# Second feed-forward layer: drains on VectorE, a longer planned way for the scale of x, seven block products from the third tile

## The chip, the cores and the metric

The kernel runs on one core of one Trainium2 chip. The metric is device time in microseconds, the median of several executions. TensorE multiplies, VectorE and ScalarE read its results from PSUM, GpSimd works on SBUF alone, and SyncE (SP) issues nearly all transfers.

## The reference, cut to what matters

```python
x = attention(q, k, v)                     # 2304 tokens x 512, fp32
h = x @ w_in;  x = (silu(h)) @ w_out       # first layer, 512 -> 2048 -> 512
h = x @ w_in2                              # second layer, the one that changes
g = np.maximum(h, 0.0) + alpha * np.minimum(h, 0.0)
out = (g @ w_out2).astype(np.float32)
```

## The kernel before

The second layer takes the 2304 tokens in nine tiles of 256 (n = 0 to 8). A tile has eight steps; a step makes 256 of the 2048 hidden values. Every fp32 operand is split into a high and a low fp16 part, and a product of two operands is three fp16 matmuls (function `three`, line 1030).

For one step, `up2` does 24 matmuls of 256 columns into one PSUM bank h (four such banks take turns: h, h, acc, acc). `act2` turns h into g: VectorE makes u (lines 1199 and 1203), ScalarE copies it to the high part of g (by the helper `act`, line 325), VectorE subtracts for the low part (line 1224). u has two buffers. `down2` multiplies g by the output weights and accumulates over the eight steps.

`down2` has two forms. The plain form (`down_plain`) takes the four 128x512 products of a step, 12 matmuls of 512 columns, into two banks. The other form (`factor`) splits g and the weights into 2x2 blocks and forms the block product from seven products in place of eight: 21 matmuls of 256 columns into four banks called e, e, s, o. It needs sums of blocks of u, four more operations on GpSimd in `act2` (line 1211), a g of 7 blocks in place of 4, and mixed output weights, which `mix_o` makes once for all tiles: a load of the kept weights by SP, four GpSimd operations (line 434), one on ScalarE and one on VectorE (line 386). The constant `PLAIN` is the first tile of the seven-product form.

At the end of a tile `store2` empties the banks ("drains" them) into the SBUF tile osb, scaled, and SP stores it. In the seven-product form that is one ScalarE copy of 256 columns and then seven VectorE operations (line 1319), each adding a bank half to osb. The plain form drains two banks, one on ScalarE and one on VectorE (line 1271). A new tile's first down needs the banks of the tile before it.

`load2` brings the next tile's x: four loads by SP into the single buffer xs, a VectorE maximum over it (line 1136), and then a maximum over the partitions. From tile 2 on that takes two transfers: `row` writes 128 single values to DRAM, `rows` reads them back to all partitions, and VectorE reduces `rows` (line 1146). After some tiny operations ScalarE and VectorE split x (line 1157) into xh, of which there are two.

Tiles 0 and 1 go through the eight steps together, while the output weights are split and kept; the others follow one by one, with the next tile's ups running some steps ahead of a tile's downs.

The order of all instructions on all engines is made ahead of time by a planner (class `Plan`). Each operation has an engine, a cost and a due time `at` in the planner's own units; the planner simulates the engines and always takes, of the operations that can start, the one with the smallest `at`. A tile buffer's turn and the dependences set what can start. The engines then work through their lists strictly in order. A transfer's planned end is:

```python
            if e == "DMA":
                dma_free = max(dma_free, start + min(o.cost, 0.63) + 0.65) + o.extra
                o.end = dma_free + 0.95
```

where the cost is 0.5 and `extra` the size in KB divided by 350. In `act2` and `down2` due times advance by `STEP2` = 0.85 a step.

Of the kernel before, what the change touches and what calls it, by code (L numbers as in the profile page):

```python
# [13 lines left out]
AF = mybir.ActivationFunctionType  # L14
ALU = mybir.AluOpType
# [21 lines left out]
FIRST_LOAD = (-20.0, -6.9)  # L37
EYE = -19.85
AHEAD = 4
DOWN2, STEP2, STEP_FIRST, G_PLACES = 3.0, 0.85, 1.8, 3  # L40
TOGETHER2, PLAIN, FIRST_DOWN = 2, 3, 1.8


SLACK, SPARE2, SWITCH = 0.56, 0.3, 1.0
# [188 lines left out]
def dve2_cost(n, pointers=0, shared=False):  # L233
    return (155 + 60 * pointers + n / 0.96) * (1.1 if shared else 1.0) * 1e-3
# [15 lines left out]
def block_causal_attention_silu_prelu(  # L250
# [14 lines left out]
    nc = tc.nc  # L265
# [3 lines left out]
    NT, DM = out.shape  # L269
# [6 lines left out]
    N2 = NT // T2  # L276
    assert (S, DM, PAIRS) == (576, 512, 4)

    plan = Plan()
    add = plan.add  # L280
# [6 lines left out]
    psum = ctx.enter_context(tc.tile_pool(name="psum", bufs=1, space=PSUM))  # L287
# [28 lines left out]
    def dma(dst, src, kib, reads=(), writes=(), after=()):  # L316
        return add("DMA", 0.5, lambda: nc.sync.dma_start(dst(), src()), reads, writes, kib / 350.0, after)
# [809 lines left out]
    def load2(n, after=()):  # L1127
        s = sb(ff2_p, [128, T2 // 32, KD, 32], F32, "xs")
        x2 = x2d[places[n]]
        for z in range(4):  # L1130
            add("DMA", 0.5, lambda z=z: nc.sync.dma_start(
                s()[32 * z:32 * z + 32].rearrange("p i k t -> p i (k t)"),
                x2()[:, 128 * z:128 * z + 128].rearrange("(i p) n -> p i n", p=32)),
                [x2], [(s, z)], extra=T2 / 350.0, after=after)
        sc = xsc[n] = sb(ff2_p, [128, 4], F32, "xsc", 3)
        add("DVE", dve_cost(KD * T2), lambda: nc.vector.tensor_reduce(  # L1136
            sc()[:, 0:1], s().rearrange("p i k t -> p (i k t)"), axis=AX.X, op=ALU.max, apply_absolute_value=True),
            [s], [sc])
        if n < TOGETHER2:
            spread(lambda: sc()[:, 0:1], [sc], lambda: sc()[:, 1:2], [sc])  # L1140
        else:
            row = sb(dram_p, [1, 128], F32, f"row{n}")
            rows = sb(ff2_p, [128, 128], F32, "rows")
            dma(lambda: row().rearrange("o p -> p o"), lambda: sc()[:, 0:1], 1, [sc], [row])
            dma(lambda: rows(), lambda: row().to_broadcast([128, 128]), 64, [row], [rows])
            add("DVE", dve_cost(128), lambda: nc.vector.tensor_reduce(sc()[:, 1:2], rows(), axis=AX.X, op=ALU.max),
                [rows], [sc])
        m = lambda: sc()[:, 1:2].bitcast(I32)
        tiny(m, m, 0x7F800000, None, ALU.bitwise_and, None, sc)
        tiny(m, m, float(27 << 23), float(TOP << 23), ALU.max, ALU.subtract, sc)  # L1150
        add("DVE", dve_cost(6), lambda: nc.vector.reciprocal(sc()[:, 2:3], sc()[:, 1:2]), [sc], [sc])
        t = sb(ff2_p, [128, 2, KD, T2], F16, "xh2", 2)
        for kk in range(KD):
            part = lambda e, kk=kk: t()[:, e, kk].rearrange("p (i t) -> p i t", t=32)
            act(T2, lambda part=part: part(0), lambda kk=kk: s()[:, :, kk], AF.Copy, [s, sc], [(t, (0, kk))],
                scale=lambda: sc()[:, 2:3])
            add("DVE", dve_cost(T2, 1, 1), lambda part=part, kk=kk: nc.vector.scalar_tensor_tensor(  # L1157
                part(1), s()[:, :, kk], sc()[:, 2:3], part(0), op0=ALU.mult, op1=ALU.subtract),
                [s, sc, (t, (0, kk))], [(t, (1, kk))])
        for kind in "io":  # L1160
            if kind in wsc:
                add("DVE", dve_cost(1, 1, 1), lambda kind=kind: nc.vector.tensor_scalar(
                    sc()[:, 1:2], sc()[:, 1:2], wsc[kind]()[:, 2:3], 2.0**(G_EXP if kind == "i" else 0),
                    op0=ALU.mult, op1=ALU.mult), [sc, wsc[kind]], [sc])
        tiny(lambda: sc()[:, 3:4], lambda: sc()[:, 1:2], -1.0, None, ALU.mult, None, sc)
        xh2[n] = t
# [99 lines left out]
    def store_plain(n):  # L1266
        sc = xsc[n]
        e = sb(ff2_p, [128, 2, DM], F32, "osb", 2)
        for t, a in enumerate(acc.pop(n)):
            if t:  # L1270
                add("DVE", dve2_cost(DM, 1), lambda a=a: nc.vector.tensor_scalar(
                    e()[:, 1], a(), sc()[:, 1:2], None, op0=ALU.mult), [a, sc], [(e, t)])
            else:
                act(DM, lambda: e()[:, 0], lambda a=a: a(), AF.Copy, [a, sc], [(e, t)], psum=True,
                    scale=lambda: sc()[:, 1:2])
            row = 0
            for r0, count in rows_of(2 * places[n] + t):
                dma(lambda r0=r0, count=count: out[r0:r0 + count],
                    lambda row=row, count=count, t=t: e()[row:row + count, t], count * 2, [(e, t)])
                row += count  # L1280
# [18 lines left out]
    def store2(n):  # L1299
        if n < PLAIN:  # L1300
            return store_plain(n)
        sc = xsc.pop(n)
        banks = acc.pop(n)
        e = sb(ff2_p, [128, 2, DM], F32, "osb", 2)
        c11, c12, c21, c22 = ((j, half) for j in range(2) for half in range(2))
        at = lambda c: lambda: e()[:, c[0], 256 * c[1]:256 * c[1] + 256]

        def part(i):
            bank, half = SLOTS_OF[i]
            return (banks[bank], half), lambda: banks[bank]()[:, 256 * half:256 * half + 256]  # L1310

        key, m1 = part(0)
        act(256, at(c11), m1, AF.Copy, [key, sc], [(e, c11)], psum=True, scale=lambda: sc()[:, 1:2])
        for i, col, base, dst in (
            (5, 1, c11, c22), (3, 3, c22, c21), (4, 1, c22, c12), (4, 1, c21, c22), (2, 1, c11, c11), (1, 3, c21, c21),
            (6, 3, c12, c12),
        ):
            key, m = part(i)
            add("DVE", dve2_cost(256, 1), lambda m=m, col=col, base=base, dst=dst: nc.vector.scalar_tensor_tensor(  # L1319
                at(dst)(), m(), sc()[:, col:col + 1], at(base)(), op0=ALU.mult, op1=ALU.add),  # L1320
                [key, sc, (e, base)], [(e, dst)])
            for j in range(2):
                if i != {0: 6, 1: 1}[j]:
                    continue
                row = 0
                for r0, count in rows_of(2 * places[n] + 1 - j):
                    dma(lambda r0=r0, count=count: out[r0:r0 + count],
                        lambda row=row, count=count, j=j: e()[row:row + count, j], count * 2,
                        [(e, c) for c in ((c11, c12), (c21, c22))[j]])
                    row += count  # L1330
# [3 lines left out]
    for k, j in enumerate(jobs):  # L1334
        start = START[k] if k < len(START) else 2.0 * (k - PAIRS) - LEAD
        for t, f in j.steps():
            at = start + t
            if k < FIRST * PAIRS and t == LOAD:
                at = FIRST_LOAD[k // PAIRS] + 0.1 * k
# [106 lines left out]
    for s in range(half + 1):  # L1446
        base = total + 1 + STEP_FIRST * s
        if s < half:
            for m in order2[2 * s:2 * s + 2]:
                plan.at = base - 1.0  # L1450
                load_w(1, "o", m, scanned)
                plan.at = base
                split_w(1, "o", m)
            for n in range(TOGETHER2):
                plan.at = base + 0.4 * n
                up2(n, s)
                act2(n, s)
            if s == 3:
                load2(TOGETHER2, after=stores[-2:])
        elif low_parts:  # L1460
            low_parts.pop()(())
        if s:
            for n in range(TOGETHER2):
                plan.at = base + FIRST_DOWN + 0.4 * n
                down2(n, s - 1)
    for n in range(TOGETHER2):
        store2(n)
    for k in range((N2 - TOGETHER2) * half + 1):
        n, s = divmod(k, half)
        n += TOGETHER2  # L1470
        base = after_first + STEP2 * k
        if n < N2:
            plan.at = base
            up2(n, s)
            act2(n, s)
            if n == TOGETHER2:
                plan.at = base + 1.0
                mix_o(s)
            if s == 1 and n + 1 < N2:
                load2(n + 1)  # L1480
        elif low_parts:
            low_parts.pop()(())
        if k >= 1:
            pn, s = divmod(k - 1, half)
            plan.at = base + DOWN2 + (SWITCH - 0.4 * s if s < 3 else 0.0)
            down2(pn + TOGETHER2, s)
            if s == half - 1:
                store2(pn + TOGETHER2)

    with tc.manual_schedule():  # L1490
# [86 lines left out]
```

## Time and profile before

| | |
|---|---|
| median of 3 runs | 913.66 us (913.22 to 916.06) |
| the profiled execution | 913.75 us |
| its span, first to last instruction | 912.0 us |
| TensorE busy | 97% of the span |
| VectorE, ScalarE, GpSimd busy | 76%, 51%, 29% |
| mean granted TensorE clock | 0.996 of 2.4 GHz |

The profile is of one execution, and its times count from the first instruction. The second layer's matmuls begin at about 529 us. A busy share is an average over the whole span; what a change in the second layer is worth has to be read from that stretch. Matmul ends in the trace are modelled, so a pace is read from start to start.

### The profile page before, as it was taken

How to read it: one execution, taken by the hardware profiler on the slowest of the kernel's cores; microseconds unless marked ns; L12 is line 12 of the kernel's file. 1: busy time of each engine (PE TensorE's matmuls, PEld its weight loads, DVE VectorE, ACT ScalarE, POOL GpSimd, SP SyncE). 2: the span in 40 equal slices, each digit the busy share in tenths (PEclk: the TensorE clock that was granted, in tenths of full speed). 3: DMA queues.
4: the chain of work that ended last, by engine and by line, in shares of the span. 5: the costliest groups of instructions: out<-in, count | busy, mean ns of one | idle time of the engine just before them, and what ended most of it. 6: DMA issues, size and time to landing. Idle time of an engine off the chain costs nothing. (4 is left out here: it accounts for less than half of the span.)

```text
span 912.0 us, 18221 instructions
## 1 busy us (share of the span) xinstructions
PE 885.8 (97%) x6845; PEld 741.3 (81%) x6845; DVE 694.3 (76%) x1557; ACT 465.2 (51%) x1070; POOL 263.5 (29%) x380
## 2 busy tenths in 40 slices
PE   7899999999999999999999999999989999999997
PEld 5688888898988888889788786667658888888886
DVE  5999767688888888887489897896575856757673
ACT  6987556677868777775236753342122222213121
POOL 6501002232212222221000000572044544536552
PEclk9999999999999999999999999999999999999999
DMA  9952134487665766659698981441110110100010
GB/s 316 407 215 53 35 94 110 110 145 151 123 162 119 155 134 130 151 134 251 222 327 321 268 282 42 142 160 47 27 50 4 47 28 24 28 28 1 24 24 24
DMA packets 134248, 116.55 MB, mean 128 GB/s; under 512 B 100240, under 2 KB 111504, under 8 KB 134160
## 3 DMA queue, kind: packets, MB, share of 16 engines
q1 hardware_dynamic: 133008, 111.19, 44.4%
q0 software_dynamic: 1152, 4.19, 1.1%
q8 instruction: 54, 0.88, 0.5%
q14 instruction: 34, 0.28, 0.1%
HBM read 78.65 MB, written 14.16 MB: 102 GB/s over the span
## 5 line engine op out<-in xcount | busy, mean ns | idle before, releaser
L1030 PE MATMUL h<-x_all,w0i 128*128 128x256 f32 (+1 forms) x1440 | 224.7, 308 | 2.4 <-ACT x_all L325 1.5
L1030 PEld LDWEIGHTS h<-x_all,w0i 128*128 128x128 f32 x1440 | 199.8, 191 | 22.9 <-issue 3.8
L1030 PEld LDWEIGHTS <-w1i 128*128 128x128 f16 x1728 | 168.9, 98 | 24.7 <-issue 0.5
L325 ACT ACTIVATE g<-u 128x896 f16<-128x896 f32 (+1 forms) x72 | 60.7, 843 | 223.6 <-POOL u L1211 112.0
L1030 PEld LDWEIGHTS <-g 128*128 128x128 f16 x1296 | 127.2, 98 | 51.9 <-issue 8.5
L1030 PE MATMUL acc<-w0o,g 128*128 128x512 f32 x672 | 168.8, 394 | 0.2
L1211 POOL TENSOR_TENSOR u<-u 128x128 f32<-128x128 f32 x192 | 116.6, 628 | 162.9 <-DVE u L1203 75.6
L1030 PEld LDWEIGHTS acc<-w0o,g 128*128 128x128 f32 x672 | 122.4, 188 | 27.5 <-issue 2.5
L1030 PE MATMUL acc<-xh,w1i 128*128 128x256 f16 x864 | 100.0, 273 | 0.0
L335 POOL TENSOR_TENSOR g<-t,g 128x512 fp32r<-128x512 f32 x40 | 53.0, 1326 | 161.7 <-ACT g L325 157.7
L1030 PE MATMUL h<-xh,w1i 128*128 128x256 f16 x864 | 99.4, 273 | 0.0
L1224 DVE SCALAR_TENSOR_TENSOR g<-u,g 128x896 f16<-128x896 f32 (+1 forms) x72 | 74.1, 1030 | 12.7 <-ACT g L325 12.6
L325 ACT ACTIVATE p<-p,stat 128x512 f16<-128x512 f32 (+2 forms) x112 | 63.3, 608 | 22.0 <-issue 7.7
L1030 PE MATMUL e<-w1op,g 128*128 128x512 f16 (+1 forms) x336 | 67.6, 333 | 3.9 <-ACT osb L325 2.6
L325 ACT ACTIVATE p<-e,stat 128x256 f32<-128x256 f32 (+2 forms) x98 | 51.0, 527 | 33.2 <-DVE stat L946 22.3
L325 ACT ACTIVATE t<-h 128x512 f32<-128x512 f32 x72 | 43.0, 597 | 44.4 <-PE h L1030 37.7
L1030 PE MATMUL e<-w1om,g 128*128 128x256 f16 x432 | 56.6, 275 | 4.8 <-DVE osb L1319 4.2
L1075 DVE SCALAR_TENSOR_TENSOR t<-t,h 128x512 f32<-128x512 f32 x72 | 49.0, 680 | 13.7 <-ACT t L325 12.5
L325 ACT ACTIVATE g<-t 128x512 fp32r<-128x512 f32 x72 | 45.4, 630 | 19.5 <-DVE t L1075 19.0
L885 DVE SCALAR_TENSOR_TENSOR p<-p,stat,p 128x384 f16<-128x384 f32 (+1 forms) x64 | 48.4, 796 | 4.4 <-ACT p L325 4.1
L1030 PE MATMUL e<-w0o,g 128*128 128x512 f32 x192 | 49.4, 393 | 0.0
L416 POOL DMA_DIRECT2D kept<-wso x8 | 4.8, 602 | 136.2 <-DVE wso L371 70.3
(167 smaller groups left out, 1336.1 us busy)
## 6 DMA issues: line engine op xcount, KB each, us to landing
st<-qkv_b SPq DMA_DIRECT2D x16, 800.0 KB, 4.8
raw0i<-w_in SPq DMA_DIRECT2D x16, 512.0 KB, 9.9
raw0o<-w_out SPq DMA_DIRECT2D x16, 512.0 KB, 9.9
scano<-w_out SPq DMA_DIRECT2D x16, 512.0 KB, 6.6
raw1i<-w_in SPq DMA_DIRECT2D x16, 512.0 KB, 5.3
raw1o<-w_out SPq DMA_DIRECT2D x16, 512.0 KB, 5.9
scani<-w_in SPq DMA_DIRECT2D x13, 512.0 KB, 4.4
x<-x2e SPq DMA_DIRECT2D x18, 256.0 KB, 2.4
```

The costliest lines, as they stand in the source:

```text
L325: nc.scalar.activation(dst(), src(), func, **k)
L335: eng.tensor_tensor(lo(), src(), hi().bitcast(F32), op=ALU.subtract)
L416: add("POOL", 1.5, lambda: nc.gpsimd.dma_start(kept[s](), both().rearrange("p c n -> p (c n)")), [a, b], [kept[s]])
L885: add("DVE", dve_cost(n, 1, 1), lambda hl=hl, rr=rr, pr=pr: nc.vector.scalar_tensor_tensor(hl()[:, :, 1], pr(), rr(), hl()[:, :, 0], op0=A ...
L1030: nc.tensor.matmul(dst, lhs(a), rhs(b), start=(start and n == 0), stop=(stop and n == 2))
L1075: add("DVE", dve_cost(2 * T1), lambda: nc.vector.scalar_tensor_tensor(t(), t(), 1.0, h3(), op0=ALU.add, op1=ALU.mult), [t, h], [t])
L1211: add("POOL", pool2_cost(128, 2.5), lambda out_=out_, x=x, y=y, op=op: nc.gpsimd.tensor_tensor(u()[:, out_], u()[:, x], u()[:, y], op=op), ...
L1224: add("DVE", dve2_cost(blocks * 128, 0, True), lambda: nc.vector.scalar_tensor_tensor(side(1)(), src(), 2.0**-G_EXP, side(0)(), op0=ALU.mu ...
```

## The change

Five things change, all in the second layer.

`PLAIN` goes from 3 to 2, so tile 2 takes the seven-product form. Since it now needs the mixed weights, the calls of `mix_o` move out of the loop over tile 2 and ahead of it, with an earlier due time each (`MIX`).

The transfer `rows` is booked with 2600 KB in place of 64; the transfer itself stays as it is. Only the planner sees the number.

`load2` of the next tile is called at a tile's step 0 and not at step 1.

Every drain is VectorE's: the plain form's ScalarE copy and the first operation of the seven-product form become VectorE operations.

The due times of the drains are 8.0 units (tiles 0 and 1) and 5.0 units (the others) earlier.

```diff
-DOWN2, STEP2, STEP_FIRST, G_PLACES = 3.0, 0.85, 1.8, 3
-TOGETHER2, PLAIN, FIRST_DOWN = 2, 3, 1.8
+DOWN2, STEP2, STEP_FIRST, G_PLACES, MIX = 3.0, 0.85, 1.8, 3, 6.0
+TOGETHER2, PLAIN, FIRST_DOWN = 2, 2, 1.8
...
-            dma(lambda: rows(), lambda: row().to_broadcast([128, 128]), 64, [row], [rows])
+            dma(lambda: rows(), lambda: row().to_broadcast([128, 128]), 2600, [row], [rows])
...
         for t, a in enumerate(acc.pop(n)):
-            if t:
-                add("DVE", dve2_cost(DM, 1), lambda a=a: nc.vector.tensor_scalar(
-                    e()[:, 1], a(), sc()[:, 1:2], None, op0=ALU.mult), [a, sc], [(e, t)])
-            else:
-                act(DM, lambda: e()[:, 0], lambda a=a: a(), AF.Copy, [a, sc], [(e, t)], psum=True,
-                    scale=lambda: sc()[:, 1:2])
+            add("DVE", dve2_cost(DM, 1), lambda a=a, t=t: nc.vector.tensor_scalar(
+                e()[:, t], a(), sc()[:, 1:2], None, op0=ALU.mult), [a, sc], [(e, t)])
...
-        act(256, at(c11), m1, AF.Copy, [key, sc], [(e, c11)], psum=True, scale=lambda: sc()[:, 1:2])
+        add("DVE", dve2_cost(256, 1), lambda: nc.vector.tensor_scalar(
+            at(c11)(), m1(), sc()[:, 1:2], None, op0=ALU.mult), [key, sc], [(e, c11)])
...
                 plan.at = base + FIRST_DOWN + 0.4 * n
                 down2(n, s - 1)
+    plan.at -= 8.0
     for n in range(TOGETHER2):
         store2(n)
+    for s in range(half):
+        plan.at = after_first + STEP2 * s - MIX
+        mix_o(s)
     for k in range((N2 - TOGETHER2) * half + 1):
...
             up2(n, s)
             act2(n, s)
-            if n == TOGETHER2:
-                plan.at = base + 1.0
-                mix_o(s)
-            if s == 1 and n + 1 < N2:
+            if s == 0 and n + 1 < N2:
                 load2(n + 1)
...
             down2(pn + TOGETHER2, s)
             if s == half - 1:
+                plan.at -= 5.0
                 store2(pn + TOGETHER2)
```

## Rows read from the trace of the kernel before

**Rows 1.** The page's first part, TensorE: busy us, share, instructions.

```profile
PE 885.8 (97%) x6845; PEld 741.3 (81%) x6845; DVE 694.3 (76%) x1557; ACT 465.2 (51%) x1070; POOL 263.5 (29%) x380
```

**Rows 2.** Waits of TensorE, 640 to 912 us: total us, times, longest.

```profile
PE e L1030 <- DVE osb L1319: 4.2, 4, 1.5
...
PE e L1030 <- DVE g L1224: 1.3, 1, 1.3
```

**Rows 3.** TensorE's timeline: start, us, instructions; plain and seven-product steps.

```profile
638.88 5.34 PE L1030 MATMUL e<-w1op,g 128*128 128x512 f16 x24
644.06 2.78 PE L1030 MATMUL acc<-xh,w1i 128*128 128x256 f16 x24
...
883.52 0.49 PE L1030 MATMUL e<-w1op,g 128*128 128x256 f16 x3
...
885.81 2.78 PE L1030 MATMUL acc<-xh,w1i 128*128 128x256 f16 x24
```

**Rows 4.** TensorE's timeline at the end of tile 2; in brackets idle time before.

```profile
667.52 0.59 PE L1030 MATMUL e<-w1op,g 128*128 128x512 f16 x2
...
671.58 5.40 PE L1030 MATMUL h<-xh,w1i 128*128 128x256 f16 x48
679.63 0.49 PE L1030 MATMUL e<-w1op,g 128*128 128x256 f16 x3 [2.64 <-ACT osb L325]
...
681.12 1.44 PE L1030 MATMUL e<-w1om,g 128*128 128x256 f16 x6 [0.54 <-DVE osb L1271]
...
683.94 2.78 PE L1030 MATMUL acc<-xh,w1i 128*128 128x256 f16 x24
```

**Rows 5.** The stretch 677 to 684 us: length, busy us by engine, clock, DMA.

```profile
677.00:684.00 7.00, 3.83 (x22) 2.70 (x22) 6.73 (x11) 2.48 (x3) 3.46 (x5) 0.76 0.21 75
```

**Rows 6.** TensorE's timeline at the end of tile 3.

```profile
720.95 0.49 PE L1030 MATMUL e<-w1op,g 128*128 128x256 f16 x3
...
722.07 0.82 PE L1030 MATMUL e<-w1om,g 128*128 128x256 f16 x6 [0.31 <-DVE osb L1319]
...
723.84 2.78 PE L1030 MATMUL acc<-xh,w1i 128*128 128x256 f16 x24
```

**Rows 7.** Waits of VectorE, 540 to 912 us: the longest in total.

```profile
DVE xsc L1146 <- DMA rows<-row: 54.4, 7, 9.9
```

**Rows 8.** Timelines of SP's queue and of VectorE: one scale's way.

```profile
682.41 0.33 SPq L317 DMA_DIRECT2D row<-xsc  x1
...
690.17 0.33 SPq L317 DMA_DIRECT2D rows<-row  x1
...
694.91 0.29 DVE L1146 TENSOR_REDUCE xsc<-rows 128x1 f32<-128x128 f32 x1 [8.30 <-DMA rows<-row]
```

**Rows 9.** Timelines of VectorE and ScalarE near the end of tile 3.

```profile
709.15 0.88 DVE L1199 TENSOR_SCALAR u<-h,alpha_sb 128x256 f32<-128x256 f32 x2
...
715.94 0.88 DVE L1199 TENSOR_SCALAR u<-acc,alpha_sb 128x256 f32<-128x256 f32 x2
...
718.40 0.46 ACT L325 ACTIVATE osb<-e,xsc 128x256 f32<-128x256 f32 x1
718.89 0.49 DVE L1319 SCALAR_TENSOR_TENSOR osb<-e,xsc,osb 128x256 f32<-128x256 f32 x1 [1.35 <-ACT osb L325]
```

**Rows 10.** Timeline of VectorE: the last drain of tile 7.

```profile
881.22 0.47 DVE L1319 SCALAR_TENSOR_TENSOR osb<-s,xsc,osb 128x256 f32<-128x256 f32 x1
```

**Rows 11.** Timelines: last mixed weights, tile 2's first down, GpSimd's first sums.

```profile
621.80 1.28 DVE L386 SCALAR_TENSOR_TENSOR w1om<-v,wsco,w1om 128x1024 f16<-128x1024 f32 x1 [2.01 <-ACT w1om L325]
...
633.67 2.75 PE L1030 MATMUL e<-w1op,g 128*128 128x512 f16 x12
...
668.27 2.60 POOL L1211 TENSOR_TENSOR u<-u 128x128 f32<-128x128 f32 x4 [47.69 <-ACT xh L325]
```

**Rows 12.** Timelines of ScalarE and VectorE at the very end.

```profile
904.68 0.47 ACT L325 ACTIVATE osb<-e,xsc 128x256 f32<-128x256 f32 x1 [3.58 <-PE e L1030]
905.19 1.47 DVE L1319 SCALAR_TENSOR_TENSOR osb<-e,xsc,osb 128x256 f32<-128x256 f32 x3 [2.96 <-ACT osb L325]
```

## The prediction
> **What bounds the kernel now.** I read the page first. TensorE is busy 885.8 of 912.0 us [rows 1], so what can be won is idle time of TensorE, or work of its own. The list of who waited for whom comes next. From 640 us on TensorE waits in only seven places over 0.2 us: four times for VectorE's drains of a finished tile (4.2 us together), once 1.3 us for a VectorE g [rows 2], and at one tile end 2.64 us for a ScalarE drain with 0.54 us for a VectorE one right behind it [rows 4]. All lie at tile ends of the second layer, so I read TensorE's timeline there.
>
> The paces first. In the plain form two down steps take 644.06 − 638.88 = 5.18 us, 2.59 us each; in the seven-product form one takes 885.81 − 883.52 = 2.29 us [rows 3]. The busy figure exceeds the pace by 5.34 − 5.18 = 0.16 us, because the last matmul's modelled end outlasts it; so a row of 48 up matmuls of 5.40 us is 5.24 us of pace, two steps of 2.62.
>
> The end of tile 2, the third tile and today's last plain one, costs twice. Its last down begins at 667.52 and the next work at 671.58: 4.06 us for 2.59 of pace, 1.47 lost. From 671.58 to 683.94 lie two up steps and the first seven-product down: 12.36 − 5.24 − 2.29 = 4.83 lost [rows 3, 4]. Waits explain 2.64 + 0.54 = 3.18 of this; the mean granted clock of 677 to 684 us is 0.76 [rows 5], so part of that stretch ran at the 1.2 GHz level and the rest at 2.4, after TensorE had stood 2.64 us.
>
> The ends of tiles 3 to 6 look alike. At the first of them the down takes 723.84 − 720.95 = 2.89 us, 0.60 over pace, 0.31 of it the listed wait [rows 6]. I take the other 0.29 for each of the four: 4.2 + 4 × 0.29 = 5.36 us. Together the six places lose 1.47 + 4.83 + 5.36 = 11.66 us.
>
> Why are the drains late? VectorE's waits answer: seven times, 54.4 us in all, it stands for the broadcast of x's scale [rows 7]. One case: the row is issued at 682.41, its broadcast at 690.17, and VectorE's reduction runs at 694.91 after 8.30 us idle: a way of 12.5 us [rows 8]. The planner books 0.5 + 0.65 + 0.95 us and KB/350 for a transfer, hence 2.1 + 0.2 + 2.3 = 4.6 us for the way, and so orders the reduction some 8 us too early on an engine that works in order. All u and g work behind it slips. It catches up slowly: two u buffers circulate, and from the u begun at 709.15 to the one begun two steps later at 715.94 it is 6.79 us, 3.4 per step against TensorE's 2.62 + 2.29 = 4.91. A slip of 8.3 us at a gain of 1.5 per step needs some 5.5 steps, 27 us, from 695 to 722: exactly the tile's end, where the drains should run. There ScalarE's first drain comes at 718.40, and VectorE has idled 1.35 us for it at 718.89 [rows 9]. The counter-example is the end of tile 7, during which no x is loaded: the last drain begins at 881.22, TensorE's new down at 883.52, and there is no wait [rows 3, 10].
>
> **Part by part.** *Seven for eight products in tile 2.* Eight down steps save 2.59 − 2.29 each: 2.4 us. The cost is 8 × 2.60 us of GpSimd sums, where GpSimd stood idle 47.69 us; the row that shows this is the first such sum of tile 3. Larger g tiles add 0.3 to 0.4 us per step to ScalarE and VectorE. The mixed weights must be there when tile 2's first down starts, 633.67; today the last of the eight is done at 623.08, and the last is needed only some 35 us after that start [rows 11]. So the order of the eight mixes, brought forward by MIX, is priced at nothing: they run in the first phase already, their eight loads on SP's queue stand ahead of tile 3's x either way, and the cover is at least 10 us. If it were gone, TensorE would wait one for one.
>
> *Longer planned way of the scale.* 2600/350 = 7.43 us are booked for the broadcast, so the way is planned at 0.5 + 0.65 + 0.95 + 0.2 + 0.5 + 0.65 + 7.43 + 0.95 = 11.8 us, against the 12.5 measured. The reduction is then ordered behind two more steps of u and g; of some 8 us per tile about 1 stays, and TensorE's four up buffers, 4 × 4.91 us, cover it. Next late would be x itself, which is loaded nearly two tiles ahead. The transfers planned behind it are shifted in the plan too, but the weights' loads are issued before.
>
> The Trainium skill, "DMA: Bandwidth & Descriptors", section "Anatomy of one DMA — SWDGE (gpsimd) path", speaks against this edit: it gives a DMA about 2.0 us fixed plus bytes/436 GB/s, some 4.2 us for the two as an estimate, which the old plan fits. By it there would be no wait to remove and the sum would end near 905.1; the 12.5 us of this trace decide.
>
> *x a step sooner.* Four x loads, the row and the broadcast go 4.9 us earlier in SP's order, perhaps past the two stores of the tile just ended. SP stands on the row's landing for 7.8 us with the stores behind it; nobody reads these. Priced at nothing, at most 0.2 us.
>
> *Drains on VectorE, five to eight planner units sooner* (a step of 4.91 us is 0.85 units, so 29 to 46 us). ScalarE gives up one 0.46 us drain per tile, VectorE takes it at 0.49 [rows 9], and the hand-over from a ScalarE queue that itself waits for GpSimd's sums disappears. Eight drains at about 0.4 us of pace are 3.3 us; TensorE's two up steps at each end hide 5.24. So I remove all 11.66 us, lower bound nothing, since the drains could stay late. Behind a drain that waits for its product stand the next tile's u and g; four steps of up lead hide that.
>
> The Trainium skill, "VectorE: DVE Perf Modes", section "Specifications", puts ScalarE closer to PSUM, which speaks for leaving it there. By the rows the difference is 0.03 us per drain, 0.2 over the kernel, on an engine that has room.
>
> *The very end.* ScalarE's drain begins at 904.68 and VectorE's next at 905.19 [rows 12]; a VectorE drain of 0.4 us pace in its place ends about there. 0 ± 0.2 us.
>
> **Sum**, from the profiled execution's 913.75 us (span 912.0 and 1.75 around it; the median of the runs is 913.66, so both serve): 913.75 − 11.66 − 2.4 = 899.7. I leave 0.2 us in each of the six places, as no list shows shorter waits: 1.2. Forecast 900.9 us.
>
> **Rivals.**
> 1. *The drains stay late at the four ends* because something else keeps VectorE behind: GpSimd's four sums, which take 2.6 us per step, also sit in the chain of each u buffer, and the new plan may still order drains behind g's that wait for them. For it: those sums are the longest part of the 6.79 us that two steps take with two u buffers [rows 9, 11], and no edit shortens them. Against: tile 7's end, which had the same sums [rows 10]. 899.7 + 5.36 = 905.1; with tile 2's new end as bad as its old one, up to 909.9. Chance 0.21. The page's 2 us rule has its time here, and no more than 0.01 of it.
> 2. *Only the products change:* the planner's order at the ends comes out as before, for example because ready times and not priorities set it. 913.75 − 2.4 = 911.4. Against: the booked way alone changes ready times. Chance 0.08.
> 3. *Slower: VectorE parks on the drains.* With such early priorities a drain is ordered as soon as the plan has its product; where TensorE on the chip is later than in the plan, VectorE stands with all u and g behind it. Today's parks, up to 9.9 us, cost 1.34 us on average at the next end; past the lead of four steps, 19.6 us, every further microsecond stalls TensorE. At 22 us for each of eight drains it costs 8 × 2.4 = 19 us, and with today's losses gone 900 + 19 = 919. Against: TensorE's paces hardly vary. Chance 0.05.
>
> **Numbers.** The forecast has 0.66; its own range is 898.8 (0.9 below the sum, for the very end, the spread of the runs below their median, 0.4, and a better tile 2) to 903. Within 0.3%, 2.7 us, a measurement of this kernel can't tell a change. Taking in most of the first rival, the range is 898.8 to 907.5. Faster by over 0.3% (below 910.9) is the forecast and rival 1, 0.87; within it rival 2, 0.08; slower rival 3, 0.05.
>
> **What would show it.** Tile 2's downs in 256-column matmuls on four banks; VectorE's wait for the broadcast down from 54.4 us to under 15; no ScalarE drain; each tile's eight drains done before the next tile's first down; tile starts 39.3 us apart (8 × 4.91), not 39.3 + 5.36/4 = 40.6; a granted clock of 1.00 from 660 on. It is wrong if TensorE's list of waits still names a drain for over 2 us, or shows a wait for mixed weights in tile 2, or VectorE's list a wait for TensorE's last products of many microseconds.

## The result and the profile after

The changed kernel takes 899.39 us (median of 4 runs, 898.29 to 899.61) against 913.44 us for the kernel before (912.96 to 916.06); the ratio is 0.9838, 95% interval 0.9818 to 0.9858. Forecast were 900.9 us, with 898.8 to 907.5 as the range. The median lies 0.6 us inside the low end; by the ratio, 0.9838 × 913.44 = 898.6 us, it lies 0.2 below it, and the interval of the ratio is 1.8 us wide to either side. The profiled execution took 899.29 us with a span of 897.5.

The page's first part after the change, TensorE (it was [rows 1]):

```profile
PE 879.7 (98%) x6917; PEld 747.7 (83%) x6917; DVE 702.9 (78%) x1572; ACT 463.7 (52%) x1061; POOL 281.6 (31%) x412
```

TensorE is busy for 6 us less, and 72 more matmuls are in the trace: tile 2 does 21 short ones a step for 12 long ones.

To keep the first layer out of the comparison, I use one measure throughout, **the stretch**: from the start of tile 0's first down to the start of the last group of products. In the timeline of TensorE, of the kernel before:

```profile
546.06 2.75 PE L1030 MATMUL e<-w1op,g 128*128 128x512 f16 x12
...
906.44 0.82 PE L1030 MATMUL o<-w1op,g 128*128 128x256 f16 x6
```

and of the changed kernel, with the ends of tiles 2 and 3 between (they answer to [rows 4] and [rows 6]):

```profile
545.62 2.75 PE L1030 MATMUL e<-w1op,g 128*128 128x512 f16 x12
...
667.29 5.40 PE L1030 MATMUL h<-xh,w1i 128*128 128x256 f16 x48
672.53 0.49 PE L1030 MATMUL e<-w1op,g 128*128 128x256 f16 x3
...
674.83 2.78 PE L1030 MATMUL acc<-xh,w1i 128*128 128x256 f16 x24
...
706.59 5.40 PE L1030 MATMUL h<-xh,w1i 128*128 128x256 f16 x48
711.83 0.49 PE L1030 MATMUL e<-w1op,g 128*128 128x256 f16 x3
...
714.13 2.78 PE L1030 MATMUL acc<-xh,w1i 128*128 128x256 f16 x24
...
891.96 0.82 PE L1030 MATMUL o<-w1op,g 128*128 128x256 f16 x6
```

The stretch falls from 360.38 to 346.34 us, by 14.04; the prediction's terms were 11.66 + 2.4 = 14.06. No row of it carries a bracket: TensorE no longer waits over 0.2 us anywhere in the stretch. The first down of tile 4 starts 711.83 − 672.53 = 39.30 us after that of tile 3, eight times 4.91, and takes 714.13 − 711.83 = 2.30 us.

Where [rows 5] had a clock of 0.76, the stretch after tile 2 now reads (length, busy us of TensorE, its weight loads, VectorE, ScalarE, GpSimd, then clock, DMA, GB/s):

```profile
672.00:679.00 7.00, 7.00 (x67) 6.29 (x65) 6.01 (x11) 1.90 (x2) 5.01 (x8) 1.00 0.33 77
```

VectorE's waits from 540 us on (total us, times, longest) have turned around; the wait for the broadcast was 54.4 us in [rows 7]:

```profile
DVE u L1199 <- PE acc L1030: 45.3, 19, 4.3
DVE u L1199 <- PE h L1030: 14.8, 12, 2.3
...
DVE osb L1309 <- PE e L1030: 3.5, 7, 2.5
...
DVE xsc L1146 <- DMA rows<-row: 2.7, 2, 1.5
```

VectorE now waits for TensorE, as the engine that is ahead should. The way of a scale has not become shorter; SP's queue and VectorE's timeline, to be read beside [rows 8]:

```profile
677.72 0.34 SPq L317 DMA_DIRECT2D row<-xsc  x1
684.95 0.34 SPq L317 DMA_DIRECT2D rows<-row  x1
...
691.28 0.28 DVE L1146 TENSOR_REDUCE xsc<-rows 128x1 f32<-128x128 f32 x1
```

The reduction has no bracket: VectorE came to it, 13.6 us after the row's issue, when the data had landed. And the drains of tile 3 (in VectorE's timeline, beside [rows 9]) start with the tile's last products and end before the next down at 711.83:

```profile
705.16 0.48 DVE L1309 TENSOR_SCALAR osb<-e,xsc 128x256 f32<-128x256 f32 x1 [0.17 <-PE e L1030]
...
708.90 0.47 DVE L1316 SCALAR_TENSOR_TENSOR osb<-s,xsc,osb 128x256 f32<-128x256 f32 x1
```

What lies outside the stretch hardly differs: 0.44 us less ahead of it, where TensorE's instructions are the same in both kernels, and 897.5 − 891.96 = 5.54 us behind it against 912.0 − 906.44 = 5.56.

### The profile page after: what moved, and what is told of

It is laid out like the page before. It is cut to its first block, busy times and chain, and to the rows that moved or that the text cites. A ratio compares the mean times of both kernels' runs of the same rounds, so it can differ in the third digit from the quotient of the medians.

```text
span 897.5 us, 18422 instructions
## 1 busy us (share of the span) xinstructions
PE 879.7 (98%) x6917; PEld 747.7 (83%) x6917; DVE 702.9 (78%) x1572; ACT 463.7 (52%) x1061; POOL 281.6 (31%) x412
## 4 chain that ended last, share of the span: by engine, by line
PE 59%; DMA 4%; DVE 3%; SPq 1%; issue 1%; ACT 1%; POOL 0%; DVEq 0%; ACTq 0%
PE h L1030 18%; PE acc L1030 17%; PE e L1030 12%; PE s L1030 5%; PE o L1030 3%; DMA scani<-w_in 2%; PE e L734 2%; PE o L908 1%; SPq L1131 1%; DMA scano<-w_out 1%; DMA xs<-x 1%; DMA raw1o<-w_out 1%; PE s L734 1%; PE o L918 0%; ACT p L325 0%
## 5 line engine op out<-in xcount | busy, mean ns | idle before, releaser
L1211 POOL TENSOR_TENSOR u<-u 128x128 f32<-128x128 f32 x224 | 136.5, 629 | 129.4 <-DVE u L1203 104.5
L325 ACT ACTIVATE g<-u 128x896 f16<-128x896 f32 (+1 forms) x72 | 63.2, 878 | 207.7 <-POOL u L1211 141.3
L1030 PEld LDWEIGHTS <-g 128*128 128x128 f16 x1368 | 133.9, 98 | 32.8
L1224 DVE SCALAR_TENSOR_TENSOR g<-u,g 128x896 f16<-128x896 f32 (+1 forms) x72 | 76.0, 1056 | 12.2 <-ACT g L325 12.2
L1199 DVE TENSOR_SCALAR u<-acc,alpha_sb 128x256 f32<-128x256 f32 x72 | 32.5, 479 | 46.3 <-PE acc L1030 45.3
L1030 PE MATMUL e<-w1om,g 128*128 128x256 f16 x504 | 64.2, 273 | 0.0
L1030 PE MATMUL e<-w1op,g 128*128 128x256 f16 (+1 forms) x264 | 49.5, 311 | 0.0
```

The costliest lines, as they stand in the source:

```text
L325: nc.scalar.activation(dst(), src(), func, **k)
L1030: nc.tensor.matmul(dst, lhs(a), rhs(b), start=(start and n == 0), stop=(stop and n == 2))
L1199: add("DVE", dve2_cost(T2, 1), lambda c=c, m=m: nc.vector.tensor_scalar(u()[:, 2 * c:2 * c + 2].rearrange("p i t -> p (i t)"), h()[:, T2 * ...
L1211: add("POOL", pool2_cost(128, 2.5), lambda out_=out_, x=x, y=y, op=op: nc.gpsimd.tensor_tensor(u()[:, out_], u()[:, x], u()[:, y], op=op), ...
L1224: add("DVE", dve2_cost(blocks * 128, 0, True), lambda: nc.vector.scalar_tensor_tensor(side(1)(), src(), 2.0**-G_EXP, side(0)(), op0=ALU.mu ...
```

## The experiments

The result fits the sum so well that it can't say which edit did it: the prediction gave 11.66 us to the longer way and the drains together. **Theory A**: VectorE's standing on the broadcast (its idle wait at the reduction) makes it late, and the drains are only where that shows. **Theory B**: the drains were late because of their place behind ScalarE's queue and their due times. **Theory C**, tried later: the booked 2600 KB help because they push back all later transfers in the plan.

Four kernels (numbers 1 to 4) take one edit alone to the kernel before, or leave one out of the changed kernel.

**The longer way alone.**

```diff
 # kernel before
-            dma(lambda: rows(), lambda: row().to_broadcast([128, 128]), 64, [row], [rows])
+            dma(lambda: rows(), lambda: row().to_broadcast([128, 128]), 2600, [row], [rows])
```

Expected: 

> The kernel before with one edit: the broadcast of x's scale booked with 2600 KB, the drains and tile 2 as before. Theory A (VectorE's standing on the broadcast makes it late, and the drains are only where this shows): VectorE's wait for it falls from 54.4 us to under 10, the four seven-product tile ends lose under 1 us together in place of 5.36, the 1.47 us before tile 2's end go; tile 2's own plain end may keep 1 to 2 of its 4.83. 902 to 904 us. Theory B (the drains are late because of their place, behind ScalarE's queue and with late due times): the wait falls as well, but the ends keep most of 5.36 and 4.83; 908 to 912 us.

**The drains alone.**

```diff
 # kernel before: both drain edits of the change, and
+    plan.at -= 8.0
     for n in range(TOGETHER2):
...
+                plan.at -= 5.0
                 store2(pn + TOGETHER2)
```

Expected: 

> The kernel before with the drains on VectorE and 8.0 and 5.0 units sooner; scale's way and tile 2 as before. Theory A: VectorE still stands 50 us or more on the broadcast and is late at the ends; drains ordered ahead of u and g help a part, the ends lose 2 to 5 us of 5.36; 906 to 911 us. Theory B: the ends lose under 1 us and tile 2's end under 1; 902 to 904 us.

**Seven products alone.**

```diff
 # kernel before: mix_o ahead of the loop with MIX = 6.0, and
-TOGETHER2, PLAIN, FIRST_DOWN = 2, 3, 1.8
+TOGETHER2, PLAIN, FIRST_DOWN = 2, 2, 1.8
```

Expected: 

> The kernel before with tile 2 in the seven-product form and the mixes brought forward; scale's way and drains as before. By the sum: 2.4 us of TensorE pace go. Theory A: the end of tile 2 then looks like the other four and loses 0.6 to 1.8 us in place of 4.83, the 1.47 before it may stay; 906 to 909 us. If seven products brought only the pace: 911.

**Everything but the longer way.**

```diff
 # changed kernel
-            dma(lambda: rows(), lambda: row().to_broadcast([128, 128]), 2600, [row], [rows])
+            dma(lambda: rows(), lambda: row().to_broadcast([128, 128]), 64, [row], [rows])
```

Expected: 

> The changed kernel with the broadcast booked at 64 KB again. Theory A: VectorE stands some 50 us again, the five tile ends lose 0.6 to 1.8 us each; 902 to 907 us. Theory B: under 1 us lost, 899 to 900.5 us.

Measured, with the kernel before run beside them on the same chip (908.82 us there), and the stretch from each profile:

```
                        median us   ratio to before (95%)      stretch us
longer way alone          902.47    0.9932 (0.9907 to 0.9957)    348.73
drains alone              907.29    0.9980 (0.9967 to 0.9993)    353.78
seven products alone      914.98    1.0065 (1.0039 to 1.0090)    360.86
everything but the way    911.73    1.0021 (1.0004 to 1.0039)    359.78
```

The medians are of one chip. The stretches are to be read with care: the kernel before has no profile on this chip, and its 360.38 us are those of the first profile. A fixed mark is the stretch without any listed wait, 348.73 us with eight products in tile 2 and 346.34 with seven.

One edit, a number that only the planner reads, clears all six places at once, with the drains where they were, the first still on ScalarE. In TensorE's timeline the stretch runs without a bracket from

```profile
549.25 2.75 PE L1030 MATMUL e<-w1op,g 128*128 128x512 f16 x12
...
897.98 0.82 PE L1030 MATMUL o<-w1op,g 128*128 128x256 f16 x6
```

That is 360.38 − 348.73 = 11.65 us less than in the first profile, and 908.82 − 902.47 = 6.35 us by the medians of this chip, where the kernel before has less to lose (number 12 below). Theory A expected this, and its allowance for tile 2's plain end wasn't needed.

The drains alone bring 908.82 − 907.29 = 1.5 us. They clear the four later ends too, though VectorE stands some 7.6 us in each of those tiles, so theory B is right that they can, and at those ends either edit is enough. But TensorE's timeline keeps one long wait, at the end of tile 2, and the stretch 5.05 us above the mark:

```profile
679.84 0.80 PE L1030 MATMUL e<-w1op,g 128*128 128x256 f16 x3 [3.52 <-DVE osb L1270]
```

The other two were a surprise, outside what either theory had expected. Seven products save their pace and still lose, 914.98 against 908.82 us: without the way the changed form of tile 2 is slower than the plain one. TensorE's timeline with seven products alone:

```profile
670.60 0.28 PE L1030 MATMUL e<-w1op,g 128*128 128x256 f16 x1 [3.71 <-DVE g L1224]
...
682.71 0.80 PE L1030 MATMUL e<-w1op,g 128*128 128x256 f16 x3 [2.95 <-DVE osb L1319]
...
685.35 1.44 PE L1030 MATMUL e<-w1om,g 128*128 128x256 f16 x6 [1.21 <-DVE osb L1319]
```

and with everything but the way:

```profile
643.85 0.28 PE L1030 MATMUL e<-w1op,g 128*128 128x256 f16 x1 [4.08 <-DVE g L1224]
...
680.67 0.49 PE L1030 MATMUL e<-w1op,g 128*128 128x256 f16 x3 [3.10 <-DVE osb L1316]
...
682.83 1.44 PE L1030 MATMUL e<-w1om,g 128*128 128x256 f16 x6 [1.35 <-DVE osb L1316]
```

In both, g is late already inside tile 2, during which VectorE stands twice (6.73 and 9.26 us in the first, 8.31 and 6.26 in the second). The timelines of ScalarE and VectorE show why that g is late; with seven products alone:

```profile
660.14 0.95 ACT L325 ACTIVATE g<-u 128x896 f16<-128x896 f32 x1 [4.04 <-POOL u L1211]
...
667.69 0.29 DVE L1146 TENSOR_REDUCE xsc<-rows 128x1 f32<-128x128 f32 x1 [9.26 <-DMA rows<-row]
...
669.46 1.08 DVE L1224 SCALAR_TENSOR_TENSOR g<-u,g 128x896 f16<-128x896 f32 x1
```

GpSimd's sums for this g were done and ScalarE's copy ended at 661.09, but VectorE's part stands behind the reduction in its order. With everything but the way it is the same: the copy begins at 634.08, the reduction at 641.66 after a stand of 8.31 us, the g at 642.71. So it is again the place of the reduction. Whether GpSimd's four sums for every u make the later waits longer is not tested.

The two stretches lie 14.52 and 13.44 us above the 346.34, and the listed waits are only 9.2 and 8.5 of that. Part of the rest is the clock: the mean granted clock was 0.58 and 0.60 over 682 to 690 us, after the waits at tile 2's end.

Four more undo one part of the changed kernel.

```diff
 # 5: drains as before       # 6: eight products in tile 2
-    (all drain edits)       -TOGETHER2, PLAIN, FIRST_DOWN = 2, 2, 1.8
                             +TOGETHER2, PLAIN, FIRST_DOWN = 2, 3, 1.8
 # 7: first drain on ScalarE # 8: due times as before
-    (both drain edits)      -    plan.at -= 8.0
                             -                plan.at -= 5.0
```

Expected of 5: 

> The changed kernel with the drains as before: first one on ScalarE, due times not brought forward. Theory A: with VectorE no longer late the drains come in time; under 1.5 us lost over the tile ends, 899.5 to 901 us. Theory B: the ends lose 4 us or more, 903 to 908 us.

Expected of 6: 

> The changed kernel with PLAIN back at 3, so tile 2 takes eight products in 512-column matmuls; the mixes stay early. By the sum 2.4 us more: 901.8 us. If the plain end of tile 2 costs by itself: up to 4.8 more, 903 to 906.

Expected of 7: 

> The changed kernel with the first drain of a tile on ScalarE again, due times still early. Theory A: ScalarE is no longer held up for long, within 1 us of the changed kernel, 899 to 900.5. Theory B (the hand-over from ScalarE is what counts): 901 to 905.

Expected of 8: 

> The changed kernel with all drains on VectorE and their due times as before. Theory A: within 1 us, 899 to 900.5, as VectorE has room. Theory B (the due times are what counts): 901 to 905.

```
                               median us   ratio to before (95%)      stretch us
5 all but the drains             898.84    0.9884 (0.9861 to 0.9906)    346.34
6 all but seven products         902.92    0.9932 (0.9910 to 0.9953)    348.72
7 drains early, on ScalarE       898.96    0.9891 (0.9875 to 0.9907)    346.35
8 drains late, on VectorE        899.50    0.9898 (0.9882 to 0.9913)    346.34
```

(The kernel before took 908.75 us beside them.) With the way booked right, neither the engine of the drains nor their due time is worth more than 0.01 us of stretch: theory B falls as the cause of this result. Eight products cost 348.72 − 346.34 = 2.38 us, the pace and nothing more. Numbers 1 and 6 have the same stretch, 348.73 and 348.72, though 6 has x a step sooner, the mixes ahead and the new drains: those three together are worth nothing here.

Then the size of the one edit that counts, on the kernel before:

```diff
 # 9: only the landing planned later, nothing behind it pushed back
-                o.end = dma_free + 0.95
+                o.end = dma_free + 0.95 + o.late     # 7.25 for rows, else 0
 # 10 and 11: another size
-            dma(lambda: rows(), lambda: row().to_broadcast([128, 128]), 64, [row], [rows])
+            dma(lambda: rows(), lambda: row().to_broadcast([128, 128]), 1300, [row], [rows])   # 11: 5200
```

Expected of 9: 

> The kernel before; the broadcast keeps its 64 KB, but its planned landing is 7.25 us later, without pushing back the transfers planned behind it. Stretch from the first down of tile 0 to the last products in the profile: 360.4 us before, 348.7 with the 2600 KB booked. Theory A (what counts is the place of VectorE's reduction in its order): 348.7 to 349.5. Theory C (what counts is that all later transfers, the mixes' loads among them, are planned later): 356 or more.

Expected of 10: 

> The kernel before with the broadcast booked at 1300 KB: the way is planned at 8.1 us in place of 4.6. Theory A by its catching up: VectorE stands some 4 to 5 us per tile, makes it good in 3 steps at 1.5 us each, and is in time at the tile's end: stretch 348.7 to 350. If each us of standing counts in proportion: half of the 11.65 stays, 354 to 355.

Expected of 11: 

> The kernel before with the broadcast booked at 5200 KB: the way is planned at 19.3 us against 12.5 measured. Theory A: VectorE does not stand for it at all, x is loaded early enough, stretch 348.7. If x becomes late: a wait of up matmuls for the split x, 350 to 356.

And the kernel before once more, on this chip.

Expected: 

> The kernel before once more, for a second profile on another chip, where its runs are some 5 us shorter than at first. If the first layer, whose instructions are the same, makes the difference: stretch 360 again. Theory A allows another: VectorE's standing depends on how long the scale's way takes in an execution, and tile ends lose more or less with it: 354 to 360, with the 11.65 us smaller by as much.

```
                         median us   ratio to before (95%)      stretch us   VectorE stands
9 landing only             901.39    0.9931 (0.9911 to 0.9951)    348.72         0
10 booked 1300 KB          901.14    0.9931 (0.9914 to 0.9949)    348.72        28.0
11 booked 5200 KB          902.17    0.9941 (0.9922 to 0.9959)    348.73         0
12 the kernel before       906.59    0.9989 (0.9975 to 1.0002)    354.26        48.7
```

(The kernel before took 907.58 us beside 9 to 11.) Number 9 has theory A's stretch, so theory C falls: it is the place of the reduction, and of what hangs on it, in VectorE's order. Number 10 is the sharpest: VectorE still stands seven times, 28.0 us in all, and TensorE loses nothing. From VectorE's list of waits and its timeline:

```profile
DVE xsc L1146 <- DMA rows<-row: 28.0, 7, 7.2
```

```profile
660.91 0.29 DVE L1146 TENSOR_REDUCE xsc<-rows 128x1 f32<-128x128 f32 x1 [7.17 <-DMA rows<-row]
...
687.42 0.29 DVE L1146 TENSOR_REDUCE xsc<-rows 128x1 f32<-128x128 f32 x1 [3.64 <-DMA rows<-row]
...
696.95 0.88 DVE L1199 TENSOR_SCALAR u<-h,alpha_sb 128x256 f32<-128x256 f32 x2 [0.29 <-PE h L1030]
```

By the catching-up sum a stand of 3.64 us is made good in some 2.4 steps at 1.5 us a step, 12 us; VectorE is ahead of TensorE again, and waits for its product, 9.5 us after the reduction. One of 8.30 [rows 8] needs until the tile's end. The sum isn't the whole of it, though: the stand of 7.17 us in tile 2 would by it need 23 us, past that tile's end some 14 us later, and TensorE did not wait there either. Number 11 shows the other side: booked at 19.3 us the reduction comes late enough never to wait, and x is still in time, so between 8.1 and 19.3 us of planned way nothing changes.

Number 12 shows where the kernel before, at 907 to 909 us in these runs and 913.4 at first, differs from itself. TensorE's waits in its second layer, in the timeline:

```profile
676.53 0.49 PE L1030 MATMUL e<-w1op,g 128*128 128x256 f16 x3 [1.07 <-ACT osb L325]
...
678.03 0.82 PE L1030 MATMUL e<-w1om,g 128*128 128x256 f16 x6 [0.69 <-DVE osb L1271]
...
717.93 0.81 PE L1030 MATMUL e<-w1om,g 128*128 128x256 f16 x6 [0.44 <-DVE osb L1319]
...
758.22 0.82 PE L1030 MATMUL e<-w1om,g 128*128 128x256 f16 x6 [0.70 <-DVE osb L1319]
...
798.73 0.81 PE L1030 MATMUL e<-w1om,g 128*128 128x256 f16 x6 [0.93 <-DVE osb L1319]
...
838.56 0.82 PE L1030 MATMUL e<-w1om,g 128*128 128x256 f16 x6 [0.24 <-DVE osb L1319]
```

The places are the same, the waits mostly shorter, the 1.30 us of tile 2's last down [rows 2] is gone. The row took a median of 7.2 us to land in place of 7.7, VectorE stood 48.7 us in place of 54.4, and the stretch is 354.26, 6.12 us less. That the shorter standing is the cause fits theory A but rests on these two executions; 4.2 of the 6.12 us are at tile 2's end alone. The stretch that the change saves is thus 14.04 us against the first profile and 7.92 against this one (11.66 and 5.54 of it by the longer way), and the changed kernel's own stretch of 346.34 came again to 0.01 us in numbers 5, 7 and 8.

## Why the prediction was right, and where it was off

*What bounds the kernel* held: late drains at six places, and behind them VectorE's standing on the scale's way. The 11.66 us are 360.38 − 348.72 to the last digit, by the kernels that have only the way. That size belongs to the execution that the sum was read from: in the second profile of the same kernel the places lose 354.26 − 348.72 = 5.54, and the same sum read from it would have promised 6.1 us less. *The catching up*: number 10 was back ahead in 9.5 us where 1.5 us a step gives 12, but its longest stand was harmless against the sum. *Seven products*: 2.4 forecast, 2.38 measured. *x sooner, the mixes* and *the very end* (0 ± 0.2): nothing, as priced; 5.54 against 5.56 us at the end.

*The step that failed is a term that was mis-sized, the allowance* "I leave 0.2 us in each of the six places ...: 1.2", and with it the low end, only 0.9 us below the plain sum. Nothing was left in any of the six: the stretch fell by 14.04 us where the terms without the allowance give 14.06. So the plain sum, 899.7, was the better forecast; the median came out 0.3 us lower still, with 0.44 us less ahead of the stretch. That the low end took only 0.4 us for the spread of runs was too tight: the start of tile 0's first down alone lay between 544.56 and 549.25 us in these profiles, with 3926 or 3927 matmuls in the trace ahead of it in every kernel.

*The drains* were credited with a share that they don't have. The text says that the hand-over from ScalarE "disappears" and removes "all 11.66 us" under that heading; with the way booked right it is worth 0.01 us at most, and only without it do early VectorE drains help (1.5 us by the medians).

*Rival 2's price was wrong in sign.* "Only the products change" was put at 2.4 us faster; alone they make the kernel slower by 0.65%: a g of tile 2 is caught behind the standing reduction, and the clock falls after the waits. *Rival 1*, GpSimd's sums in the chain, did not come: with the way booked right no end is late. Whether the sums add to the loss of the seven products alone stays open. *Rival 3* did not come: VectorE's wait for a tile's products is 3.5 us over seven tiles.

The rule that was weighed, the Trainium skill, "DMA: Bandwidth & Descriptors", section "Anatomy of one DMA — SWDGE (gpsimd) path", with about 2.0 us fixed, is a fit for transfers by GpSimd's path. It does not fit this pair on SP's queue: the medians are 7.1 to 7.7 us for the row and 4.1 to 4.7 for the broadcast over all profiles. The measurement decides, and booking it is the gain but for the 2.4 us of the products.

## What to carry to other kernels

In a kernel with a planned, in-order schedule a wrong latency in the plan can cost more than a slow engine, as it did here: before moving work between engines, compare each planned way with its measured one, and look where an engine stands for a transfer that it reached too early. A stand is free as long as the engine makes it good before the next point where others need it; work out that distance, stand over gain per step, before pricing it. An edit that saves time on one engine can lose more than it saves while another engine is behind, so test edits in the order in which they depend on each other. And read the size of a loss from more than one execution: here the same kernel lost 11.66 us in one and 5.54 in another.

## What the runs showed of the hardware

The write of 128 single values, 0.5 KB in all, from 128 partitions to DRAM took 7.1 to 7.7 us in the median and up to 9.1, longer than the 64 KB read back (4.1 to 4.7). Between two profiled executions of the kernel before it differed by half a microsecond in the median, and the stretch by 6.12 us; the changed kernel's stretch came again to 0.01 us with a row median of 7.1 us and of 7.3.

After TensorE's stand of 2.64 us at the end of tile 2 the mean granted clock of 7 us was 0.76 [rows 5], at first still 1.00 (677 to 680 us), then 0.57 (680 to 684); with the drains alone, after 3.52 us, it was 0.86 over 672 to 682 us; and in the second profile of the kernel before, after 1.07 us, it stayed at 1.00 over 672 to 680 us:

```profile
672.00:680.00 8.00, 6.24 (x57) 5.28 (x56) 6.79 (x10) 3.43 (x4) 5.10 (x9) 1.00 0.17 66
```

So lateness at the same place cost more than its waits in one execution, 1.47 + 4.83 = 6.30 us for 4.48 of listed waits, and little more in the other, 2.06 for 1.76 (from tile 2's last down to tile 3's second one it is 682.28 − 667.47 = 14.81 us, where number 10 takes 12.75).
